# Four two-bank PSUM tiles in a ring with dependencies by bank, and attention visits of four and three chunks, in a fused sigmoid-attention and SwiGLU kernel

## The chip, the cores and the metric

One core of a Trainium2 chip. The metric is the time on the device in microseconds (us), start of the program to its end. Each timed version was run several times, interleaved with the kernel before on the same chip.

## The reference

Sigmoid attention over 8 batches, 12 heads, 448 positions and head dimension 64, followed by a gated feed-forward block (FFN) on the 3584 tokens.

```python
scores = q @ k.T / sqrt(64) - log(448)          # per batch and head
attn   = 1 / (1 + exp(-scores))
x      = (attn @ v)  -> [3584, 768]
g      = x @ w_gate                             # 768 -> 1536
out    = (g * sigmoid(g) * (x @ w_val)) @ w_out # 1536 -> 768
```

## The kernel before

The instruction order is fixed by the program; the framework only adds the semaphores. Of the engines, TensorE does the matmuls and transposes, ScalarE (ACT in the views) the sigmoids, VectorE (DVE) the copies and products. xT is the attention output in the layout that the FFN reads, T the transposed q and k. Words used below: a *head group* n is four heads of one batch (24 groups, three to a batch). Its scores come in seven *chunks* c. A *QK tile* is the scores of one chunk: four matmuls on 64x64 tiles of the array, side by side. *PV* is the product with v of a whole group. An *FFN unit* is one gate product and one value product of six matmuls each, or the output products of one block of 128 tokens (twice twelve matmuls). Before, a visit may also fall between the two halves of a unit (the kinds g, v and o in the loop below are halves); after, only between whole units. TensorE does FFN units most of the time and breaks off for a *visit* to attention. One trip from FFN to attention and back is called a *trip*.

PSUM, the memory that TensorE writes its results to, has eight banks. Before, four of them are two score tiles of two banks, and four are single tiles that everything else shares:

```python
psA = tile_pool(name="psA", bufs=2, space=PSUM)      # score tiles, two banks each
psG = tile_pool(name="psG", bufs=4, space=PSUM)      # one bank each

def qk_tile(n, c):
    sc = psA.tile([128, 2, 512], FP32, tag="A", name="ps_sc")
    # ... four 64x64 matmuls: two halves w, two heads h2
    return sc

def sig_tile(n, c, sc):
    pt = ptp.tile([128, 2, S], FP16, tag="pt", name="pt")
    nc.scalar.activation(out=pt, in_=sc[:, :, :S], func=SIGM, bias=sb_t, scale=qkscale)

def pv(n):
    P = [psG.tile([128, S], FP32, tag="G", name=f"ps_pv{w}") for w in range(2)]
    # ... 28 64x64 matmuls, then four VectorE copies to the two xT tiles of the group

def trans_pe(n, which):                               # q or k of one group, seven transposes
    ps = psG.tile([128, C, 128], BF16, tag="G", name="ps_tr")
    # ... seven transposes, then one VectorE copy to T

def ffn1(b, f, gate):                                 # gate or value product of one unit
    ps = psG.tile([128, S], FP32, tag="G", name="ps_g" if gate else "ps_vl")
    # ... six matmuls; gate: ScalarE sigmoid s16, VectorE t1 = ps*s16; value: VectorE hT = ps*t1
# ... ffn2: twelve matmuls, one VectorE copy to osb, then a store
```

The order of the visits, and the main loop:

```python
tiles  = [(n, c) for n in range(NJ, NQ) for c in range(C)]     # C = 7, NJ = 3, NQ = 24
visits = [tiles[i:i + 2] for i in range(0, len(tiles), 2)]     # two QK tiles to a visit

def attn_step(group, pvs):
    scs = [(n, c, qk_tile(n, c)) for n, c in group]
    for n in pvs:
        pv(n)
    for n, c, sc in scs:
        sig_tile(n, c, sc)

for dur, u in units:                       # FFN work, in order
    while vi < len(visits) and tcur >= vtime[vi]:
        group = visits[vi]; vi += 1
        attn_step(group, pvs)              # pvs: groups whose last chunk is done
        for n, c in group:
            if c == 1:
                nn = n + 2
                if loaded <= nn + 1 < NQ:
                    load3(nn + 1)          # q, k, v of a later group
                if casted <= nn < NQ:
                    cast(nn, 0, nc.gpsimd); cast(nn, 1, nc.gpsimd)
                    # ... DMA transposes from group 6 on, cast of v
            if c == 5 and n + 1 < NPE:     # NPE = 6
                trans_pe(n + 1, 0); trans_pe(n + 1, 1)
    # ... one FFN unit of kind g, v or o
    tcur += dur
```

Batch 0 has no FFN to mix with: its 21 QK tiles, sigmoids and three PV run first, while weights still load in four blocks of the gate and of the value matrix.

Of the kernel before, what the change touches and what calls it, by code (L numbers as in the profile page):

```python
# [17 lines left out]
def kernel(  # L18
# [10 lines left out]
    nc = tc.nc  # L29
# [17 lines left out]
    psA = ctx.enter_context(tc.tile_pool(name="psA", bufs=2, space=bass.MemoryType.PSUM))  # L47
    psG = ctx.enter_context(tc.tile_pool(name="psG", bufs=4, space=bass.MemoryType.PSUM))
# [14 lines left out]
    make_identity(nc, idn)  # L63

# [51 lines left out]
    def trans_pe(n, which):  # L116
        t = q16.pop((n, which))
        ps = psG.tile([128, C, 128], BF16, tag="G", name="ps_tr")
        for c in range(C):
            nc.tensor.transpose(  # L120
                out=ps[:, c, :], in_=t[:, c].rearrange("p h d -> p (h d)"), identity=idn
            )
        d = qkT.tile([128, C, 128], BF16, tag=f"T{which}", name=f"T{which}_{n}")
        nc.vector.tensor_copy(out=d, in_=ps)  # L124
        qT[(n, which)] = d
# [5 lines left out]
    def qk_tile(n, c):  # L131
        sc = psA.tile([128, 2, 512], FP32, tag="A", name="ps_sc")
        qt, kt = qT[(n, 0)], qT[(n, 1)]
        for w in range(2):
            for h2 in range(2):
                r = slice(h2 * 64, h2 * 64 + 64)
                nc.tensor.matmul(  # L137
                    out=sc[w * 64:(w + 1) * 64, h2, :S],
                    lhsT=kt[r, c, w * 64:(w + 1) * 64],
                    rhs=qt[r, :, w * 64:(w + 1) * 64],  # L140
                    start=True,
                    stop=True,
                )
        return sc
# [6 lines left out]
    def pv(n):  # L151
        b, j = divmod(n, NJ)
        P = [psG.tile([128, S], FP32, tag="G", name=f"ps_pv{w}") for w in range(2)]
        vt = v16.pop(n)
        for c in range(C):
            pt = pts.pop((n, c))
            for h2 in range(2):
                for w in range(2):
                    r = slice(w * 64, w * 64 + 64)
                    nc.tensor.matmul(  # L160
                        out=P[w][h2 * 64:(h2 + 1) * 64, :],
                        lhsT=vt[r, h2, c * D:(c + 1) * D],
                        rhs=pt[r, h2, :],
                        start=(c == 0),
                        stop=(c == C - 1),
                    )
        for h2 in range(2):
            x = xtp.tile([128, S], FP16, tag="xT", name=f"xT_{b}_{2 * j + h2}")
            for w in range(2):
                nc.vector.tensor_copy(  # L170
                    out=x[w * 64:(w + 1) * 64, :], in_=P[w][h2 * 64:(h2 + 1) * 64, :]
                )
            xT[(b, 2 * j + h2)] = x
        qT.pop((n, 0))
        qT.pop((n, 1))
# [3 lines left out]
    gcur = {}  # L179

    def ffn1(b, f, gate):
        ps = psG.tile([128, S], FP32, tag="G", name="ps_g" if gate else "ps_vl")
        w = (wg16 if gate else wv16)[f // FW]
        cs = slice((f % FW) * 128, (f % FW) * 128 + 128)
        for pr in range(NP):
            nc.tensor.matmul(  # L186
                out=ps, lhsT=w[:, pr, cs], rhs=xT[(b, pr)], start=(pr == 0), stop=(pr == NP - 1)
            )
        if gate:
            s16 = tmp.tile([128, S], FP16, tag="s16", name="s16")  # L190
            nc.scalar.activation(out=s16, in_=ps, func=SIGM)  # L191
            t1 = tmp.tile([128, S], FP16, tag="t1", name="t1")
            nc.vector.tensor_tensor(out=t1, in0=ps, in1=s16, op=MULT)  # L193
            gcur[0] = t1
        else:
            if b % 2 == 0:
                hT[(b // 2, f)] = htp.tile([128, 2, S], FP16, tag="hT", name=f"hT_{b // 2}_{f}")
            nc.vector.scalar_tensor_tensor(  # L198
                out=hT[(b // 2, f)][:, b % 2, :], in0=ps, scalar=HSC, in1=gcur[0], op0=MULT, op1=MULT
            )  # L200

    osb_cur = {}

    def ffn2(b, m, half):
        hw = DM // 2
        if half == 0:
            osb_cur[0] = osp.tile([128, DM], FP32, tag="osb", name="osb")
        osb = osb_cur[0]
        o = psG.tile([128, hw], FP32, tag="G", name="ps_o")
        for f in range(NF):  # L210
            h = hT[(b // 2, f)].rearrange("p b s -> p (b s)")
            lhsT = h[:, m * 128:(m + 1) * 128]
            nc.tensor.matmul(  # L213
                out=o,
                lhsT=lhsT,
                rhs=wo16[f // FW][:, f % FW, half * hw:(half + 1) * hw],
                start=(f == 0),
                stop=(f == NF - 1),
            )
        nc.vector.tensor_scalar(  # L220
            out=osb[:, half * hw:(half + 1) * hw], in0=o, scalar1=HREC, scalar2=None, op0=MULT
        )
        if half == 1:
            for i in range(2):
                bb, c = divmod(2 * m + i, C)
                bb += b - b % 2
                dst = out[bb * S:(bb + 1) * S, :].rearrange("(p c) n -> c p n", c=C)[c]
                nc.gpsimd.dma_start(out=dst, in_=osb[i * 64:(i + 1) * 64, :])  # L228


    FU1, FU2 = 1.13, 1.95
# [3 lines left out]
    for pb in range(B // 2):  # L235
        for b in (2 * pb, 2 * pb + 1):
            f1_start[b] = tt
            for f in range(NF):
                units.append((FU1, ("g", b, f)))
                units.append((FU1, ("v", b, f)))  # L240
                tt += 2 * FU1
            f1_end[b] = tt
        for m in range(7):
            for half in range(2):
                units.append((FU2, ("o", 2 * pb + (m > 2), m, half)))
                tt += FU2
# [3 lines left out]
    tiles = [(n, c) for n in range(NJ, NQ) for c in range(C)]  # L250
    visits = [tiles[i:i + 2] for i in range(0, len(tiles), 2)]
# [10 lines left out]
    def attn_step(group, pvs):  # L262
        scs = [(n, c, qk_tile(n, c)) for n, c in group]
        for n in pvs:
            pv(n)
        for n, c, sc in scs:
            sig_tile(n, c, sc)
# [15 lines left out]
    trans_pe(0, 0)  # L283
    trans_pe(0, 1)
# [6 lines left out]
    for n, c in b0:  # L291
        attn_step([(n, c)], [n - 1] if c == 2 and n > 0 else [])
        if (n, c) == (0, 3):
            trans_pe(1, 0)
            trans_pe(1, 1)
# [5 lines left out]
        if (n, c) == (1, 3):  # L301
            trans_pe(2, 0)
            trans_pe(2, 1)
# [6 lines left out]
        if (n, c) == (2, 3):  # L310
            trans_pe(3, 0)
            trans_pe(3, 1)
# [13 lines left out]
    pend = []  # L326
    for dur, u in units:
        while vi < len(visits) and tcur >= vtime[vi]:
# [4 lines left out]
            for n, c in group:  # L333
# [18 lines left out]
                if c == 5 and n + 1 < NPE:  # L352
                    trans_pe(n + 1, 0)
                    trans_pe(n + 1, 1)
        if pend and (u[0] == "g" and u[2] == 0 and (u[1], NP - 1) not in xT or vi == len(visits) and tcur >= vtime[-1] + 4.0):
# [3 lines left out]
        if u[0] == "g":  # L359
            ffn1(u[1], u[2], True)  # L360
        elif u[0] == "v":
            ffn1(u[1], u[2], False)
        else:
            ffn2(*u[1:])
# [31 lines left out]
```

## Time and profile before

| | before |
|---|---|
| median of 3 runs | 449.37 us (448.82 to 450.17) |
| span of the profiled execution | 446.4 us |
| TensorE busy | 94% |
| VectorE, ScalarE busy | 49%, 47% |
| trips from FFN to attention and back | 74 |

The prediction shows the page's busy line, its DMA row, the chain of waits and two visits in order of time. In the page, one digit of a row is a fortieth of the span (11 us) in tenths. Here is the granted TensorE clock over the slices:

```profile
PEclk9899999999999999999999999999999999999998
```

The second digit of the clock row is an 8: in the second slice TensorE ran part of the time at half clock (from 19.3 to 22.7 us). The view by stretches of time says how slow (columns: stretch; its length; busy time of each engine with the number of instructions; granted clock; DMA share; GB/s):

```profile
19.30:22.60 3.30, 3.02 (x36) 1.79 (x35) 0.00 (x0) 2.02 (x3) 0.90 (x2) 0.50 1.17 285
```

The clock was 0.50 there.

### The profile page before, as it was taken

How to read it: one execution, taken by the hardware profiler on the slowest of the kernel's cores; microseconds unless marked ns; L12 is line 12 of the kernel's file. 1: busy time of each engine (PE TensorE's matmuls, PEld its weight loads, DVE VectorE, ACT ScalarE, POOL GpSimd, SP SyncE). 2: the span in 40 equal slices, each digit the busy share in tenths (PEclk: the TensorE clock that was granted, in tenths of full speed). 3: DMA queues.
4: the chain of work that ended last, by engine and by line, in shares of the span. 5: the costliest groups of instructions: out<-in, count | busy, mean ns of one | idle time of the engine just before them, and what ended most of it. 6: DMA issues, size and time to landing. Idle time of an engine off the chain costs nothing.

```text
span 446.4 us, 7870 instructions
## 1 busy us (share of the span) xinstructions
PE 420.9 (94%) x3252; PEld 212.2 (48%) x3252; DVE 220.1 (49%) x360; ACT 210.9 (47%) x267; POOL 100.7 (23%) x142
## 2 busy tenths in 40 slices
PE   2678999999999999999999999999999999999992
PEld 1344444444555444444555444444555545555661
DVE  1265665466334456556424546646524446555231
ACT  3887675655533655565444464565444441221000
POOL 1764140220234512000324612200021100000221
PEclk9899999999999999999999999999999999999998
DMA  8999999994284986500278694220033300000242
GB/s 264 332 286 286 182 249 196 232 280 149 58 249 94 262 248 167 164 1 1 50 222 231 135 302 134 42 42 3 0 82 87 79 4 1 1 1 0 72 106 70
DMA packets 63587, 59.88 MB, mean 134 GB/s; under 512 B 35648, under 2 KB 61760, under 8 KB 63552
## 3 DMA queue, kind: packets, MB, share of 16 engines
q1 hardware_dynamic: 52992, 41.30, 34.8%
q0 software_dynamic: 10560, 18.09, 19.3%
q8 instruction: 25, 0.41, 0.4%
q14 instruction: 10, 0.08, 0.1%
HBM read 47.19 MB, written 11.01 MB: 130 GB/s over the span
## 4 chain that ended last, share of the span: by engine, by line
PE 92%; ACT 2%; DMA 2%; DVE 1%; issue 1%; POOL 0%; SPq 0%; POOLq 0%; ACTq 0%
PE ps_o L213 25%; PE ps_vl L186 25%; PE ps_g L186 25%; PE ps_sc L137 9%; PE ps_pv L160 7%; ACT pt L148 2%; DMA st<-in_q_dram 2%; PE ps_tr L120 1%; DVE xT L170 1%; SPq L88 0%; POOL c L108 0%; DVE osb L220 0%; POOL out_dram L228 0%; POOLq L391 0%; ACTq L148 0%
## 5 line engine op out<-in xcount | busy, mean ns | idle before, releaser
L148 ACT ACTIVATE pt<-ps_sc,sb_t 128x896 f16<-128x896 f32 x168 | 159.6, 1005 | 88.5 <-PE ps_sc L137 88.5
L186 PE MATMUL ps_g<-xT,wg 128*128 128x448 f16 x576 | 125.4, 353 | 1.5 <-DVE xT L170 1.4
L186 PE MATMUL ps_vl<-xT,wv 128*128 128x448 f16 x576 | 124.9, 353 | 0.0
L213 PE MATMUL ps_o<-wo,hT 128*128 128x384 f16 x672 | 113.5, 326 | 0.0
L193 DVE TENSOR_TENSOR t<-ps_g,s 128x448 f16<-128x448 f32 x96 | 59.9, 624 | 84.7 <-ACT s L191 84.1
L191 ACT ACTIVATE s<-ps_g 128x448 f16<-128x448 f32 x96 | 52.2, 544 | 103.2 <-PE ps_g L186 103.2
L213 PEld LDWEIGHTS <-hT 128*128 128x128 f16 x672 | 64.0, 98 | 48.6 <-issue 7.9
L186 PEld LDWEIGHTS <-wv 128*128 128x128 f16 x576 | 54.3, 98 | 58.6 <-issue 10.7
L186 PEld LDWEIGHTS <-wg 128*128 128x128 f16 x576 | 54.1, 98 | 57.0 <-issue 9.7
L228 POOL DMA_DIRECT2D out_dram<-osb x56 | 29.3, 528 | 211.2 <-DVE osb L220 211.0
L170 DVE CAST xT<-ps_pv 64x448 f16<-64x448 f32 x96 | 59.7, 622 | 30.8 <-PE ps_pv L160 29.4
L198 DVE SCALAR_TENSOR_TENSOR hT<-ps_vl,t 128x448 f16<-128x448 f32 x96 | 60.0, 625 | 16.6 <-PE ps_vl L186 8.5
L220 DVE TENSOR_SCALAR osb<-ps_o 128x384 f32<-128x384 f32 x56 | 31.2, 558 | 74.6 <-PE ps_o L213 74.4
L137 PE MATMUL ps_sc<-T,T 64*64 64x448 bf16 x672 | 51.1, 370 | 8.8 <-ACT pt L148 7.2
L108 POOL CAST c<-st 128x896 bf16<-128x896 f32 x43 | 39.7, 939 | 54.7 <-DMA st<-in_q_dram 30.3
L108 POOL CAST v<-st 128x896 f16<-128x896 f32 x24 | 22.6, 942 | 72.8 <-PE ps_pv L160 52.9
L160 PE MATMUL ps_pv<-pt,v 64*64 64x448 f16 x672 | 37.5, 359 | 0.3 <-ACT pt L148 0.3
L137 PEld LDWEIGHTS <-T 64*64 64x64 bf16 x672 | 13.7, 106 | 39.7 <-issue 37.1
L160 PEld LDWEIGHTS <-v 64*64 64x64 f16 x672 | 20.8, 109 | 12.8 <-issue 0.9
L120 PE MATMUL ps_tr<-idn,c 128*128 128x128 bf16 x84 | 7.3, 250 | 6.5 <-DVE c L108 4.7
L120 PEld LDWEIGHTS <-c 128*128 128x128 bf16 x84 | 5.9, 113 | 8.8 <-DVE c L108 4.7
L124 DVE COPY T<-ps_tr 128x896 bf16<-128x896 bf16 x12 | 7.1, 620 | 5.4 <-PE ps_tr L120 5.2
(14 smaller groups left out, 17.2 us busy)
## 6 DMA issues: line engine op xcount, KB each, us to landing
st<-in_q_dram SPq DMA_DIRECT2D x24, 448.0 KB, 4.5
st<-in_k_dram SPq DMA_DIRECT2D x24, 448.0 KB, 5.9
st<-in_v_dram SPq DMA_DIRECT2D x24, 448.0 KB, 7.3
out_dram<-osb POOLq DMA_DIRECT2D x56, 192.0 KB, 3.1
wg<-in_moe_w_gate_dram POOLq DMA_DIRECT2D x4, 576.0 KB, 24.8
wv<-in_moe_w_val_dram POOLq DMA_DIRECT2D x4, 576.0 KB, 29.7
wo<-in_moe_w_out_dram POOLq DMA_DIRECT2D x4, 576.0 KB, 35.4
T<-c SPq DMA_TRANSPOSE x36, 3.2
```

Source lines behind the costliest of these rows:

```text
L108: eng.tensor_copy(out=o, in_=i)
L137: nc.tensor.matmul(out=sc[w * 64:(w + 1) * 64, h2, :S], lhsT=kt[r, c, w * 64:(w + 1) * 64], rhs=qt[r, :, w * 64:(w + 1) * 64], start=True, ...
L148: nc.scalar.activation(out=pt, in_=sc[:, :, :S], func=SIGM, bias=sb_t, scale=qkscale)
L160: nc.tensor.matmul(out=P[w][h2 * 64:(h2 + 1) * 64, :], lhsT=vt[r, h2, c * D:(c + 1) * D], rhs=pt[r, h2, :], start=(c == 0), stop=(c == C - 1),
L170: nc.vector.tensor_copy(out=x[w * 64:(w + 1) * 64, :], in_=P[w][h2 * 64:(h2 + 1) * 64, :])
L186: nc.tensor.matmul(out=ps, lhsT=w[:, pr, cs], rhs=xT[(b, pr)], start=(pr == 0), stop=(pr == NP - 1))
L191: nc.scalar.activation(out=s16, in_=ps, func=SIGM)
L193: nc.vector.tensor_tensor(out=t1, in0=ps, in1=s16, op=MULT)
L198: nc.vector.scalar_tensor_tensor(out=hT[(b // 2, f)][:, b % 2, :], in0=ps, scalar=HSC, in1=gcur[0], op0=MULT, op1=MULT)
L213: nc.tensor.matmul(out=o, lhsT=lhsT, rhs=wo16[f // FW][:, f % FW, half * hw:(half + 1) * hw], start=(f == 0), stop=(f == NF - 1),)
L220: nc.vector.tensor_scalar(out=osb[:, half * hw:(half + 1) * hw], in0=o, scalar1=HREC, scalar2=None, op0=MULT)
L228: nc.gpsimd.dma_start(out=dst, in_=osb[i * 64:(i + 1) * 64, :])
```

## The change

The intent: fewer trips. A visit of four or three QK tiles needs more than two score tiles, so the eight banks become four persistent two-bank tiles, used in turn by everybody (a ring). A user of a whole tile would hold two banks longer than needed, so users declare which bank each matmul writes and each reader reads, and a declared pair on different banks isn't ordered.

```diff
-    psA = ctx.enter_context(tc.tile_pool(name="psA", bufs=2, space=bass.MemoryType.PSUM))
-    psG = ctx.enter_context(tc.tile_pool(name="psG", bufs=4, space=bass.MemoryType.PSUM))
+    psD = ctx.enter_context(tc.tile_pool(name="psD", bufs=1, space=bass.MemoryType.PSUM))
...
+    ring = [psD.tile([128, 2, 512], FP32, tag=f"D{i}", name=f"ps_D{i}") for i in range(4)]
...
+    class Banked:
+        def __init__(self, user=None):          # takes the next tile of the ring
...
+        def write(self, ins, bank):
+            if bank is not None:
+                self.has_mm[bank] = True
+                tc.add_to_no_dep_group(self.mm[bank], ins.ins)
+                p = self.prev
+                if p is not None and p.has_rd[1 - bank] and not (self.user == "o" and p.user == "f"):
+                    tc.declare_no_dep(ins.ins, group=p.rd[1 - bank], reason="the other bank")
+        def read(self, ins, bank):
+            if bank is not None:
+                if self.has_mm[1 - bank]:
+                    tc.declare_no_dep(ins.ins, group=self.mm[1 - bank], reason="the other bank")
+                self.has_rd[bank] = True
+                tc.add_to_no_dep_group(self.rd[bank], ins.ins)
...
-        sc = psA.tile([128, 2, 512], FP32, tag="A", name="ps_sc")
+        sc = Banked().t
...
-        P = [psG.tile([128, S], FP32, tag="G", name=f"ps_pv{w}") for w in range(2)]
+        P = Banked().t
...
-    def ffn1(b, f, gate):
+    def ffn1(b, f):                             # gate and value in one tile, one bank each
+        D = Banked("f")
+        for i, w16 in enumerate((wg16, wv16)):
+            for pr in range(NP):
+                D.write(nc.tensor.matmul(out=D.t[:, i, :S], ...), i)
...
-    tiles = [(n, c) for n in range(NJ, NQ) for c in range(C)]
-    visits = [tiles[i:i + 2] for i in range(0, len(tiles), 2)]
+    visits = [[(n, c) for c in cs] for n in range(NJ, NQ) for cs in (range(4), range(4, C))]
...
     def attn_step(group, pvs):
-        scs = [(n, c, qk_tile(n, c)) for n, c in group]
-        for n in pvs:
-            pv(n)
-        for n, c, sc in scs:
-            sig_tile(n, c, sc)
+        for part in (group[:2], group[2:]):
+            scs = [(n, c, qk_tile(n, c)) for n, c in part]
+            while pvs:
+                pv(pvs.pop(0))
+            for n, c, sc in scs:
+                sig_tile(n, c, sc)
...
-                if c == 5 and n + 1 < NPE:
-                    trans_pe(n + 1, 0)
-                    trans_pe(n + 1, 1)
+                if c == 4 and n + 1 < NPE:
+                    post.append(n + 1)          # its transposes come after the next FFN unit
...
+        fn(*args)
+        while post:
+            trans_pe(post.pop())
```

(The bodies of ffn1, ffn2 and trans_pe are cut; each now writes both banks of one tile. The loops of the `D.write` call are shortened.) The score tiles declare nothing: their one sigmoid reads both banks.

## The prediction

> **What bounds the kernel now.** I read the page first (busy shares, chain), then the waits, then the order of time around single visits of attention. The page's busy line, the DMA row of its slices and the first line of the chain of work that ended last:
>
> ```profile
> PE 420.9 (94%) x3252; PEld 212.2 (48%) x3252; DVE 220.1 (49%) x360; ACT 210.9 (47%) x267; POOL 100.7 (23%) x142
> DMA  8999999994284986500278694220033300000242
> ...
> PE 92%; ACT 2%; DMA 2%; DVE 1%; issue 1%; POOL 0%; SPq 0%; POOLq 0%; ACTq 0%
> ```
>
> TensorE is busy or next in line almost throughout; the other engines are half idle. The DMA engines are saturated in slices 2 to 9 (11 us each), which matters below. So the change can win only TensorE idle time, and PE's busy share hides that. I therefore took the start times of all 3252 matmuls and compared neighbours. At full clock the pitch is 189 ns for a 128x448 matmul, 162.5 ns for 128x384, 189 ns for four 64x64 ones side by side, 56 ns for a transpose. Count times pitch gives 395.1 us. From the first matmul at 4.7 us to the last at 437.7 us lie 38.0 us more. Where they are, by the waits:
>
> ```profile
> PEld L137 <- issue: 37.1, 88, 2.5
> PEld L186 <- issue: 20.4, 54, 1.2
> ...
> PE ps_sc L137 <- ACT pt L148: 7.2, 10, 2.1
> ...
> PE ps_g L186 <- DVE xT L170: 1.4, 2, 0.9
> ```
>
> PE hardly waits for another engine; what recurs is "issue" before the first weight load after a change of matmul kind. Two visits in order of time, one with PV and one without:
>
> ```profile
> 152.88 0.14 PEld L137 LDWEIGHTS <-T 64*64 64x64 bf16 x8 [0.37 <-issue]
> 152.88 0.57 PE L137 MATMUL ps_sc<-T,T 64*64 64x448 bf16 x8
> ...
> 153.28 1.49 PE L160 MATMUL ps_pv<-pt,v 64*64 64x448 f16 x28
> 153.31 1.91 ACT L148 ACTIVATE pt<-ps_sc,sb_t 128x896 f16<-128x896 f32 x2 [0.92 <-PE ps_sc L137]
> ...
> 154.70 0.87 PEld L186 LDWEIGHTS <-wg 128*128 128x128 f16 x6 [0.36 <-issue]
> ...
> 154.82 2.54 DVE L170 CAST xT<-ps_pv 64x448 f16<-64x448 f32 x4 [1.04 <-PE ps_pv L160]
> ...
> 162.23 0.14 PEld L137 LDWEIGHTS <-T 64*64 64x64 bf16 x8 [0.37 <-issue]
> ...
> 162.73 0.87 PEld L186 LDWEIGHTS <-wg 128*128 128x128 f16 x6 [0.36 <-issue]
> ```
>
> Start to start, every visit, whatever is in it, costs 0.220 to 0.222 us beyond its matmuls: 0.094 going into 64x64 tiles, the rest coming out. There are 74 such FFN-to-attention-to-FFN trips from 38 us on: 16.35 us. One more stall lies there, 0.635 us at 76.5 us (the gate of batch 1 waits for the copies of xT). The remaining idle time is the start, before the first FFN tile.
>
> **What the Trainium skill says.** "TensorEngine Tiling (Array Packing)", Tiling Modes, Key Properties: changing the tiling mode, not just the tile, drains TensorE. The trace agrees: 0.22 us per round trip between 128x128 and 64x64, and nothing between QK and PV, which share the mode. "PSUM — Partial Sum Buffer", PSUM bank collisions: semaphores should guard PSUM by bank and quadrant; an engine may read one bank while PE writes another. The kernel before does just that with one-bank FFN tiles, so waiting by bank buys nothing over it, it only keeps what two-bank tiles would lose. The skill's first page ("Trainium Kernel Development and Optimization", Key Constraints) says that DMAs from all queues run on the same 16 engines and interleave; the saturated slices agree (332 GB/s in the best), so weights asked for earlier don't land earlier.
>
> **The change, part by part.**
> PSUM: before, two 2-bank score tiles and four 1-bank tiles; after, four 2-bank tiles used strictly in turn by QK, PV, FFN and transposes. The instruction counts per kind are the same; only order and waits move. The order of the built program shows 42 visits in place of 74. (Both also have one lone PV at the end, and in both the first visit has no FFN before it: so 74 trips before, 42 after.)
>
> 1. *Trips removed.* From 68.2 us on (why there, see 3) before has 64 trips, 14.13 us. After has the two visits of each of 18 head groups and one PV alone, 37 x 0.221 = 8.18 us. Saved 5.95 us, all on PE's path.
>
> 2. *A new wait.* A visit with PV now takes slots in the order QK0, QK1, PV, QK2, QK3, and the next FFN unit gets the slot four users back: that of QK1. The built program's semaphore says the same: that unit's first matmul waits for the sigmoid of QK1. Count from the visit's first QK matmul. In the trace above the sigmoid of QK0 starts at 0.436 (153.314-152.878), that of QK1 0.906 later, and ends 1.00 after that: 2.34. A released matmul starts 0.05 us after an activation's end (startup: 16.829 to 16.881). So the FFN can start at 2.39. Without the wait it would start at 1.829 (154.707-152.878) plus two more QK tiles, 2 x 0.189: 2.207. The wait is 0.187 us. QK3 itself needs QK0's sigmoid, done at 1.44, and PE gets there at 1.89: free. The second FFN unit takes PV's slot; the four copies end at 4.48 (157.362-152.878), release at 4.53, and PE arrives at 2.39+2.27=4.66: free, by only 0.13. QK2 needs the previous unit's last DVE read, done at 0.90, PE arrives at 1.70. The visit without PV meets slots read long before; its next FFN unit needs the gate product of the unit just before, ready about 0.3 after that unit's end, and three QK tiles take 0.79. So 18 x 0.187 = 3.37 us given back.
>    The 0.635 us stall for xT goes, since the visit before it is longer and PV follows earlier: 0.64 saved.
>
> 3. *The start.* Four score slots let QK run ahead of the sigmoids. The sigmoids of batch 0 are 21 x 0.9 = 19 us from 11.1 us on but end at 34.2 before, having waited for QK behind transposes and behind a PV at half clock. Without such waits they would end at 11.1+19 = 30.1; the ring still makes some wait for DVE's copies, so I put them near 31: about 3 us gained. But this gain is lost again, to weights. The loads of the value weights:
>
> ```profile
> L78 POOL DMA_DIRECT2D wv<-in_moe_w_val_dram x4: 826/827/845, 12.9 to 30.8; - x4
> ...
> DMA to landing us min/median/max: 18.5/29.7/36.3
> ```
>
>    The last value block lands at 30.8+36.3 = 67.1; the third at 56.4 by its semaphore. Before, their first users start at 68.22 and 57.75: margins of 1.1 and 1.4 us. After, even with no gain at the start, the third block's user would arrive at 55.9 and wait until 56.44. From there 1.14 (rest of the unit) + 0.78 (transposes) + 2.49 (visit with PV and its wait) + 4.54 (two units) + 0.79 (visit) + 1.14 (gate half) reach the last block's user at 67.3, just past its landing. So of everything that happens before 68 us, 68.22-67.3 = 0.9 us survives.
>
> Sum: 0.9 + 5.95 + 0.64 - 3.37 = 4.1 us. Against the median, 449.4-4.1 = 445.3 us, 0.9% faster. The tail is the same work as before.
>
> **The rivals.**
> *The ring stalls more than I count.* One order for all users couples PE to the slowest reader. For it: the 0.13 us margin behind PV's copies, and ScalarE gets four sigmoids in a row, so the next gate's sigmoid starts 0.3 us late. Against it: that lateness falls on a slot needed four users on, 5 us later, and DVE and ACT are about half idle. Each extra 0.2 us per visit with PV costs 3.6 us: 449, a draw.
> *No wait at all at the visits, or a cheaper one.* If PE is slower coming out of 64x64 mode, or the sigmoid is released sooner, the 3.37 us stay: 441.9. Against it: the wait adds measured stamps of one visit, and ACT is free there.
> *The start's gain survives.* If the weights land earlier because casts and loads move up, another 1 to 2 us: 443 to 444; with the previous rival 440. Against it: saturated DMA slices. The opposite is also possible: PE idling for weights for 1 to 2 us could let its clock drop. "TensorE: Matmul & The Clock Gate", Part 1, gives free-running activity windows of some 3.4 us; this trace has one at half clock from 19.3 to 22.7 us, after thinly spread QK work. Such a window costs up to 1.7 us: 447.
>
> **Range and chances.** The trips saved are near certain, so the range hangs on the new wait (0 to 0.4 us, 18 times) and the start (0 to 2.5 us). 443.0 to 447.8 should hold it 8 times in 10. Two per cent faster is under 440.4, which needs both kind rivals at once: 0.04. Two per cent slower is over 458.4, which needs over 0.7 us of extra wait at each of 18 visits: 0.02. Within: 0.94.
>
> **What would show it.** Right: PE's trips fall to 42, each still 0.22; at the FFN unit after each visit with PV, a PE wait for the sigmoid of about 0.19, 18 to 20 times, 3 to 4 us in the waits; sigmoids of batch 0 ending near 31 us; PE waiting for the third and second value blocks near 45 and 56 us; no wait for xT near 76. Wrong: waits of PE for DVE's xT copies at the second unit (then the margin of 0.13 failed), waits before QK2 or QK3, value weights landing before 55 or after 58 us, or a second half-clock window past 35 us.

## The result and the profile after

Ratios are computed as the mean time of one kernel's runs over the mean of the other's of the same rounds, so they aren't quite ratios of the medians quoted.

| | before | after |
|---|---|---|
| median (4 runs each) | 449.19 us (448.82 to 450.17) | 445.60 us (445.16 to 446.48) |
| ratio, 95% interval | | 0.9919, 0.9897 to 0.9941 |
| span of the profiled execution | 446.4 us | 443.9 us |
| trips | 74 | 42 |

It is 0.8% faster, 3.6 us by the medians. Predicted were 445.3 us and 4.1. A repeat with six runs of the unchanged changed kernel (told below) gave 445.49. The page after, busy line, clock row and the chain (in the lines of this kernel L182 is QK, L205 PV, L231 the FFN's gate and value products, L193 the score sigmoid, L162 the transposes and L169 their copies; other kernels number them a little differently):

```profile
PE 413.1 (93%) x3252; PEld 218.4 (49%) x3252; DVE 220.7 (50%) x360; ACT 208.6 (47%) x267; POOL 100.5 (23%) x142
...
PEclk9999999999999999999999999999999999999998
...
PE 75%; DMA 14%; ACT 5%; issue 2%; POOL 2%; DVE 1%; SPq 0%; POOLq 0%; ACTq 0%; DVEq 0%
```

The chain has changed: DMA was 2% of it and is 14% (9 of these are the value weights, by the chain's second line). That is the first sign that weights now stop TensorE. (The same 3252 matmuls count 7.8 us less busy than before, more than the kernel gained: their ends are modelled, so the busy share does not measure TensorE's work.) The waits after (columns: engine, line, what it waited for; us in total, times, longest):

```profile
PEld L182 <- issue: 20.6, 48, 2.3
...
PE ps_D L231 <- DMA wv<-in_moe_w_val_dram: 3.9, 3, 1.9
...
PE ps_D L182 <- DVE T L169: 2.3, 3, 1.0
...
PE ps_D L231 <- ACT pt L193: 0.4, 2, 0.2
```

"issue" before the first QK weight load of a visit was 37.1 us in 88 cases before and is 20.6 in 48: most of that are the trips that went. New are three waits for value weights and up to 1.0 us for DVE's copies of the transposes. One visit with PV, in order of time (columns: start; busy; engine, line, operation, tiles and count; idle before and its releaser):

```profile
266.53 0.57 PE L182 MATMUL ps_D<-T,T 64*64 64x448 bf16 x8
...
266.93 1.49 PE L205 MATMUL ps_D<-pt,v 64*64 64x448 f16 x28
266.96 3.70 ACT L193 ACTIVATE pt<-ps_D,sb_t 128x896 f16<-128x896 f32 x4 [0.92 <-PE ps_D L182]
...
268.73 1.04 PEld L231 LDWEIGHTS <-wg 128*128 128x128 f16 x6 [0.36 <-issue]
268.92 1.29 PE L231 MATMUL ps_D<-xT,wg 128*128 128x448 f16 x6
```

From the first QK matmul to the first FFN matmul are 268.92 - 266.53 = 2.39 us. The prediction had 2.39 with the new wait and 2.207 without it. Note how badly the wait shows: the weight load before it says only "issue 0.36", as it does in visits that don't wait, and the waits list has none of it, except for the fourth line shown above and a like one at the output units (two cases each, 0.8 us together). These are the four visits where ScalarE had been idle and began its first sigmoid 0.50 us after QK's start, not 0.436. I had to take the start times of all matmuls, as for the prediction. Excess over the matmuls' own pitch, start to start:

| visit | before | after |
|---|---|---|
| without PV | 0.219 to 0.221 us | 0.220 to 0.221 us |
| with PV | 0.221 to 0.222 us | 0.406 to 0.409 us, four of 0.466 to 0.469 (the lone PV at the end: 0.221) |

So the new wait is 0.187 us. The second FFN unit did not wait for PV's copies, and the 0.635 us for xT at 76.5 us is gone.

To tell the start from the rest, I took one mark in every trace: the first value matmul of the last weight block. Time from the mark to the last matmul:

| | mark at | mark to last matmul |
|---|---|---|
| before, first profile and repeat | 68.15, 69.61 us | 369.58, 369.59 us |
| after, first profile and repeat | 68.99, 69.00 us | 366.25, 366.24 us |

From the mark on, the change gave 3.33 to 3.34 us, and this part repeats to 0.01 us; predicted were 5.95 + 0.64 - 3.37 = 3.22. The agreement is in part luck. By the start times the visits gave 14.126 - 11.762 = 2.36 us (2.58 predicted; the four of 0.466 make the difference) and the xT stall 0.64. One QK tile more lies behind the mark in the changed kernel, which takes 0.19 back, and 0.52 us came from gaps of at most 0.011 us between FFN matmuls, 0.82 us in all before and 0.30 after, which nobody predicted and nothing here explains. Before the mark there is no dependable gain: against the first profile of before the changed kernel was 0.8 us later, against the second 0.6 earlier. The timed medians, 3.6 us, leave some 0.3 us for it. Predicted were 0.9.

Where does the start's gain go? The changed kernel began its first FFN matmul at 33.04 us (before 34.90). Then:

```profile
56.62 1.31 PE L231 MATMUL ps_D<-xT,wv 128*128 128x448 f16 x6 [1.90 <-DMA wv<-in_moe_w_val_dram]
57.76 0.94 PE L162 MATMUL ps_D<-idn,c 128*128 128x128 bf16 x14
...
58.51 1.15 DVE L169 COPY T<-ps_D 128x896 bf16<-128x896 bf16 x2
...
59.70 0.57 PE L182 MATMUL ps_D<-T,T 64*64 64x448 bf16 x8 [1.00 <-DVE T L169]
```

TensorE waits for a value block (1.90 us here, 1.71 at 44.45 us, both as predicted), and then for something not predicted: the transposes of group 5 lie directly before the QK tiles that need them, so QK waits for DVE's two copies. Start to start it cost 1.07 us. The change itself put them there. The kernel before has them directly behind a visit, with a whole unit between them and their QK, which waits for nothing:

```profile
55.66 0.95 PE L120 MATMUL ps_tr<-idn,c 128*128 128x128 bf16 x14
...
58.82 0.57 PE L137 MATMUL ps_sc<-T,T 64*64 64x448 bf16 x8
```

### The profile page after: what moved, and what is told of

Its sections match the earlier page's. It is cut to its first block, busy times and chain, and to the rows that moved or that the text cites. A ratio compares the mean times of both kernels' runs of the same rounds, so it can differ in the third digit from the quotient of the medians.

```text
span 443.9 us, 7927 instructions
## 1 busy us (share of the span) xinstructions
PE 413.1 (93%) x3252; PEld 218.4 (49%) x3252; DVE 220.7 (50%) x360; ACT 208.6 (47%) x267; POOL 100.5 (23%) x142
## 4 chain that ended last, share of the span: by engine, by line
PE 75%; DMA 14%; ACT 5%; issue 2%; POOL 2%; DVE 1%; SPq 0%; POOLq 0%; ACTq 0%; DVEq 0%
PE ps_D L231 44%; PE ps_D L258 25%; DMA wv<-in_moe_w_val_dram 9%; ACT pt L193 5%; PE ps_D L182 4%; DMA st<-in_v_dram 3%; DMA st<-in_q_dram 2%; PE ps_D L205 2%; POOL v L147 1%; DVE t L240 0%; DVE hT L244 0%; POOL wg L117 0%; ACT s L238 0%; SPq L127 0%; POOL c L147 0%
## 5 line engine op out<-in xcount | busy, mean ns | idle before, releaser
L193 ACT ACTIVATE pt<-ps_D,sb_t 128x896 f16<-128x896 f32 x168 | 156.0, 1008 | 91.7 <-PE ps_D L182 91.7
L231 PE MATMUL ps_D<-xT,wv 128*128 128x448 f16 x576 | 124.7, 353 | 3.9 <-DMA wv<-in_moe_w_val_dram 3.9
L231 PE MATMUL ps_D<-xT,wg 128*128 128x448 f16 x576 | 124.8, 353 | 1.8 <-ACT pt L193 0.4
L258 PE MATMUL ps_D<-wo,hT 128*128 128x384 f16 x672 | 111.7, 326 | 0.8 <-ACT pt L193 0.4
L240 DVE TENSOR_TENSOR t<-ps_D,s 128x448 f16<-128x448 f32 x96 | 59.8, 623 | 89.3 <-ACT s L238 87.7
L238 ACT ACTIVATE s<-ps_D 128x448 f16<-128x448 f32 x96 | 52.6, 548 | 101.1 <-PE ps_D L231 95.2
L231 PEld LDWEIGHTS <-wv 128*128 128x128 f16 x576 | 56.1, 98 | 57.2 <-DMA wv<-in_moe_w_val_dram 5.2
L231 PEld LDWEIGHTS <-wg 128*128 128x128 f16 x576 | 54.8, 98 | 59.1 <-issue 11.3
L215 DVE CAST xT<-ps_D 64x448 f16<-64x448 f32 x96 | 59.7, 622 | 30.4 <-PE ps_D L205 29.4
L269 DVE TENSOR_SCALAR osb<-ps_D 128x384 f32<-128x384 f32 x56 | 31.2, 558 | 72.9 <-PE ps_D L258 72.1
L244 DVE SCALAR_TENSOR_TENSOR hT<-ps_D,t 128x448 f16<-128x448 f32 x96 | 60.0, 625 | 12.5 <-PE ps_D L231 2.3
L182 PE MATMUL ps_D<-T,T 64*64 64x448 bf16 x672 | 47.0, 366 | 7.3 <-DVE xT L215 4.3
L205 PE MATMUL ps_D<-pt,v 64*64 64x448 f16 x672 | 36.1, 350 | 1.6 <-ACT pt L193 1.0
L182 PEld LDWEIGHTS <-T 64*64 64x64 bf16 x672 | 16.4, 107 | 29.8 <-issue 20.6
L205 PEld LDWEIGHTS <-v 64*64 64x64 f16 x672 | 20.1, 107 | 14.2 <-issue 3.0
L162 PE MATMUL ps_D<-idn,c 128*128 128x128 bf16 x84 | 7.5, 249 | 7.0 <-DVE c L147 4.9
L162 PEld LDWEIGHTS <-c 128*128 128x128 bf16 x84 | 6.2, 111 | 9.3 <-DVE c L147 5.2
L169 DVE COPY T<-ps_D 128x896 bf16<-128x896 bf16 x12 | 7.1, 620 | 2.4 <-PE ps_D L162 2.3
```

Of the source, the lines that this page charges most:

```text
L182: nc.tensor.matmul(out=sc[w * 64:(w + 1) * 64, h2, :S], lhsT=kt[r, c, w * 64:(w + 1) * 64], rhs=qt[r, :, w * 64:(w + 1) * 64], start=True, ...
L205: nc.tensor.matmul(out=P[h2 * 64:(h2 + 1) * 64, w, :S], lhsT=vt[r, h2, c * D:(c + 1) * D], rhs=pt[r, h2, :], start=(c == 0), stop=(c == C ...
L215: nc.vector.tensor_copy(out=x[w * 64:(w + 1) * 64, :], in_=P[h2 * 64:(h2 + 1) * 64, w, :S])
L231: nc.tensor.matmul(out=D.t[:, i, :S], lhsT=w16[f // FW][:, pr, cs], rhs=xT[(b, pr)], start=(pr == 0), stop=(pr == NP - 1),),
L238: D.read(nc.scalar.activation(out=s16, in_=D.t[:, 0, :S], func=SIGM), 0)
L240: D.read(nc.vector.tensor_tensor(out=t1, in0=D.t[:, 0, :S], in1=s16, op=MULT), 0)
```

## The experiments

Ratios are to the kernel before in the same rounds. Its medians were 449.06 us with experiments 1 to 4, 449.02 with 5 to 8 and 449.35 with 9 to 12. Experiments 1 to 8 ran on one chip, 9 to 12 on another, so times of the two groups are compared by their ratios.

The record has the mean granted clock of every timed run, also of those without a trace. In the fourteen profiled executions it tells how many half-clock stretches of 3.4 us there were: 0.995 to 0.997 with none, 0.991 to 0.993 with one, 0.987 with two (0.994, which none of them has, is counted as none below). It doesn't tell where they lay.

### 1. Release the score tile by halves

Theory: the 0.187 us are a wait of the FFN unit's gate for the whole sigmoid of QK1. If that sigmoid becomes two instructions, one per bank, each declared to its bank, the gate can start after the first.

```diff
-    def sig_tile(n, c, sc):
+    def sig_tile(n, c, D, split=False):            # qk_tile returns the Banked object
         pt = ptp.tile([128, 2, S], FP16, tag="pt", name="pt")
-        nc.scalar.activation(out=pt, in_=sc[:, :, :S], func=SIGM, bias=sb_t, scale=qkscale)
+        if split:
+            for i in range(2):
+                D.read(nc.scalar.activation(out=pt[:, i, :], in_=D.t[:, i, :S],
+                                            func=SIGM, bias=sb_t, scale=qkscale), i)
+        else:
+            nc.scalar.activation(out=pt, in_=D.t[:, :, :S], func=SIGM, bias=sb_t, scale=qkscale)
     def attn_step(group, pvs):
+        split = bool(pvs) and len(group) == 4
...
-                sig_tile(n, c, sc)
+                sig_tile(n, c, sc, split and c == 1)
```

> The changed kernel, with the sigmoid of QK1 in each visit with PV cut in two, one instruction for each PSUM bank, and the next FFN unit's gate waiting for the first alone. Theory (the 0.187 us at these visits is the wait for the whole sigmoid of QK1): the first half ends about 0.4 us earlier, the gate no longer waits, a visit with PV costs 0.22 us beyond its matmuls in place of 0.407, and the second unit now meets the 4.53 us release of PV's slot 0.06 us early: 18 x 0.187 less some 12 x 0.06 = 2.6 us, so 445.6 - 2.6 = 443.0 us (3.4 us, 442.2, if that second wait doesn't come). Rival (the extra is TensorE's own cost of a longer visit with PV between two lots of QK): still 0.407 us, 445.6 us.

Measured: 441.24 us (440.66 to 444.45, 6 runs), ratio 0.9849 (0.9813 to 0.9885), result correct. The visit of above, now in this kernel:

```profile
263.19 0.57 PE L183 MATMUL ps_D<-T,T 64*64 64x448 bf16 x8
...
264.53 1.15 ACT L197 ACTIVATE pt<-ps_D,sb_t 128x448 f16<-128x448 f32 x2
...
264.92 0.55 PE L183 MATMUL ps_D<-T,T 64*64 64x448 bf16 x8
...
265.40 1.31 PE L241 MATMUL ps_D<-xT,wg 128*128 128x448 f16 x6
```

Two ScalarE instructions of half the size take the place of one, and QK to FFN is 265.40 - 263.19 = 2.21 us in place of 2.39. All visits with PV after the mark are back at 0.222 us. Because TensorE arrives earlier at the second unit, 14 of these units (12 after the mark) now wait 0.043 to 0.047 us for PV's copies: the 0.13 us margin of the prediction less the 0.187 us gained is -0.06. From the mark to the end the kernel takes 363.40 us, 2.85 less than the changed one. This settles the new wait: mechanism and size. About 1.5 us more than that came from before the mark. In the profiles the mark came 1.41 us earlier (67.58 in place of 68.99): 0.86 because the third value block landed at 55.7 us in place of 56.6, 0.42 because the last one (65.8 in place of 68.9) wasn't waited for, and 0.13 from the split itself. Nothing shows that the split made the blocks land earlier: the unchanged repeat (experiment 11) has them at 54.1 and 63.5 us.

### 2 and 3. Take the weights' arrival away

Theory: the start's gain is lost to the landing of the weights. In both kernels all weight blocks of the gate and the value are made block 0, which lands first. The result is wrong (relative error 1.2253).

```diff
-    wg16 = [one.tile([128, NP, FW * 128], FP16, tag=f"wg{i}", name=f"wg16_{i}") for i in range(NW)]
-    wv16 = [one.tile([128, NP, FW * 128], FP16, tag=f"wv{i}", name=f"wv16_{i}") for i in range(NW)]
+    wg16 = [one.tile([128, NP, FW * 128], FP16, tag="wg0", name="wg16_0")] * NW
+    wv16 = [one.tile([128, NP, FW * 128], FP16, tag="wv0", name="wv16_0")] * NW
...
     def w_load(kind, i):
+        if kind != "o" and i > 0:
+            return
```

> The changed kernel, wrong on purpose: only the first block of the gate and value weights is loaded, and all FFN units use it. Same instructions on TensorE, six weight loads of 576 KB x 2 fewer. Theory (before 69 us it is the landing of the value weights that sets the pace, and eats what the start gained): the three waits of 1.87, 2.07 and 0.42 us go, 4.4 us in all, 441.2 us. Rival (the start itself, or the clock, sets the pace there): no more than 1 us faster, 444.6 to 445.6 us.

> The kernel before, with the same edit, wrong on purpose. Theory (there the weights land 1.1 to 2 us ahead of their use, so nothing waits for them): within 0.5 us of the kernel before, 448.7 to 449.7 us. So the changed kernel would be ahead of it by 8 us where weights are no limit, against 3.6 us where they are. Rival (the saturated DMA slows the start of both alike): as much faster as the changed kernel with this edit, 4 us, 445 us.

Measured: changed kernel 444.94 us (443.04 to 446.36, 6 runs), ratio 0.9912 (0.9881 to 0.9944); kernel before 447.81 us (446.55 to 449.92, 6 runs), ratio 0.9982 (0.9950 to 1.0014), nothing that its interval tells from zero. The theory falls short: with no weights to wait for, the changed kernel gains hardly anything, as the rival had it. The trace says what took their place:

```profile
57.20 0.62 DVE L242 TENSOR_TENSOR t<-ps_D,s 128x448 f16<-128x448 f32 x1 [2.75 <-ACT s L240]
...
58.47 1.15 DVE L171 COPY T<-ps_D 128x896 bf16<-128x896 bf16 x2
...
59.67 0.57 PE L184 MATMUL ps_D<-T,T 64*64 64x448 bf16 x8 [2.25 <-DVE T L171]
...
60.08 2.33 PE L207 MATMUL ps_D<-pt,v 64*64 64x448 f16 x28
```

TensorE waits 2.25 us for the copies of the transposes. These stand on VectorE behind the two products of the FFN unit just before, and the first product waits for ScalarE's gate sigmoid; only then come the copies. Then the PV takes 2.33 us in place of 1.49: half clock, as the view by stretches shows for this run.

```profile
60.60:64.00 3.40, 3.40 (x35) 1.40 (x24) 1.52 (x3) 2.59 (x4) 0.93 (x1) 0.50 1.07 287
```

The clock is 0.50 there, and also from 29.9 to 33.3 us: two stretches of 3.4 us, each worth up to half of that, 1.7 us (an estimate). So there are two limits one behind the other: weights, and the transposes' place in the order. My second theory: both have to go.

### 4. The ring alone

Rival: the gain is the ring's, not the visits'. The changed kernel with the old visits of two QK tiles:

```diff
-    visits = [[(n, c) for c in cs] for n in range(NJ, NQ) for cs in (range(4), range(4, C))]
+    tiles = [(n, c) for n in range(NJ, NQ) for c in range(C)]
+    visits = [tiles[i:i + 2] for i in range(0, len(tiles), 2)]
...
-                if c == 4 and n + 1 < NPE:
+                if c == 5 and n + 1 < NPE:
```

> One part of the change alone: the ring of four two-bank tiles with waits by bank and undivided FFN units, but the 74 visits of two chunks of the kernel before. Theory (the ring by itself gives nothing past the start, the visits saved are the gain): trips cost 0.22 us 74 times again, no wait for the sigmoid of QK1 since the next unit then gets the slot of an FFN unit, 448.5 to 449.3 us. Rival (the ring's freer slots are the gain): 446 us or less.

Measured: 450.85 us (449.30 to 451.84, 6 runs), ratio 1.0044 (1.0016 to 1.0072). The rival falls: with 74 trips of 0.22 us the ring costs time. From the mark to the end it needs 371.69 us, 2.1 more than before. In the trace are stalls for xT of 0.65 and 1.11 us between 78 and 81 us (0.635 in one place before) and one boundary at which two visits fell together, four QK in a row with 0.83 us. Expected were 448.5 to 449.3 us, no slower than before: the stalls were not foreseen.

### 5. The visits alone

The kernel before, with its old pools, and the new visits:

```diff
-    tiles = [(n, c) for n in range(NJ, NQ) for c in range(C)]
-    visits = [tiles[i:i + 2] for i in range(0, len(tiles), 2)]
+    visits = [[(n, c) for c in cs] for n in range(NJ, NQ) for cs in (range(4), range(4, C))]
...
     def attn_step(group, pvs):
-        scs = [(n, c, qk_tile(n, c)) for n, c in group]
...
+        for part in (group[:2], group[2:]):
+            scs = [(n, c, qk_tile(n, c)) for n, c in part]
+            while pvs:
+                pv(pvs.pop(0))
+            for n, c, sc in scs:
+                sig_tile(n, c, sc)
```

> The other part of the change alone: visits of four chunks with PV and three without, on the PSUM pools of the kernel before (two 2-bank score tiles, four 1-bank tiles). Theory (the larger visits need the ring's third and fourth score slot): the third chunk of a visit waits for the sigmoid of the first. Without PV that is 1.49 us after the visit's start where TensorE is ready at 0.38: 1.11 us, 21 times. With PV the fourth chunk waits for the sigmoid of the second, 2.39 against 1.89: 0.5 us, 20 times. 33 us of new waits against 7.1 us of saved trips: 449 + 26 = 475 us, 470 to 480. Rival (the visits alone give the gain, the ring is not needed): 442 to 446 us.

Measured: 476.60 us (476.25 to 476.81, 4 runs), ratio 1.0619 (1.0581 to 1.0657). A line of its waits, and the fourth QK tile of a visit:

```profile
PE ps_sc L137 <- ACT pt L148: 36.3, 53, 2.1
```

```profile
166.03 0.38 PE L137 MATMUL ps_sc<-T,T 64*64 64x448 bf16 x4 [0.31 <-ACT pt L148]
```

With two score tiles, each further QK waits for a sigmoid of about 1 us: 36.3 us in 53 cases. Visits without PV cost 1.34 to 1.44 us each, with PV 0.72 to 0.83; expected were 0.22 with 1.11 and with 0.5 us of waits, that is 1.33 and 0.72. The change is of the kind where neither half is worth anything alone: the ring pays nothing, the visits pay only with the ring.

### 6. The ring without the declarations by bank

```diff
         def write(self, ins, bank):
+            return
...
         def read(self, ins, bank):
+            return
```

> The changed kernel without its declarations by bank: each wait is for the whole two-bank tile. The built program then has the gate's sigmoid wait for the value matmuls and the next user of a slot for the last of its readers. Theory: after each visit without PV the next FFN unit waits for the last product of the unit just before, ready at 1.98 us after the visit's start where TensorE is ready at 0.69: 1.3 us at some 15 visits and 0.6 at 6 between output units; visits with PV lose 0.3 to 0.5 us more: 20 + 4 + 7 = about 28 us, 473 us, 465 to 480. Rival (four slots are enough for whole-tile waits): within 2 us of the changed kernel.

Measured: 470.88 us (470.52 to 472.34, 4 runs), ratio 1.0498 (1.0464 to 1.0532). A visit without PV:

```profile
155.30 0.76 PE L184 MATMUL ps_D<-T,T 64*64 64x448 bf16 x12
155.41 0.54 ACT L240 ACTIVATE s<-ps_D 128x448 f16<-128x448 f32 x1 [4.62 <-PE ps_D L233]
...
156.64 0.62 DVE L246 SCALAR_TENSOR_TENSOR hT<-ps_D,t 128x448 f16<-128x448 f32 x1
...
157.32 1.30 PE L233 MATMUL ps_D<-xT,wg 128*128 128x448 f16 x6 [1.26 <-DVE hT L246]
```

The gate's sigmoid starts only after the whole unit (155.41, after the value's last matmul), so the chain sigmoid, product, product ends at 157.26, and the next unit, whose slot this is, waits for it: 1.546 us for this visit (expected 0.22 + 1.3). The declarations are thus worth 470.9 - 445.6 = 25 us in this ring. They keep the ring from losing to the one-bank tiles of before, as the prediction had it.

### 7. Weights aliased and the transposes first

Second theory: put the transposes before the FFN unit in place of after it, as in the kernel before, so that DVE's copies lie beside that unit. First without weights to wait for (wrong result), so that nothing else is in the way:

```diff
-        fn(*args)
         while post:
             trans_pe(post.pop())
+        fn(*args)
```

> The changed kernel with one block of gate and value weights for all units (wrong on purpose, as before), and with TensorE's transposes of the next head group placed before the FFN unit they follow in the changed kernel. The run with the weights alone taken away came to 444.9, not 441.2: its trace has QK waiting 2.3 us at 57 us for VectorE's copies of transposes issued just before it, and a half-clock window of 3.4 us right after. Theory (two limits in a row at the start: weights, then these copies): with both gone 444.9 - 2.3 - up to 1.7 for the clock: 441.5 us, 440.5 to 442.5. Rival (a third limit takes their place): 444 us or more.

Measured: 441.52 us (440.14 to 442.72, 6 runs), ratio 0.9833 (0.9804 to 0.9862): as expected to 0.1 us, and 3.4 us under experiment 2, from the order of two statements: in the trace the 2.25 us wait and the half-clock stretch behind it are gone (the one at 30 us is still there). The mark comes at 66.51 us and the rest takes 366.24 us, as in the changed kernel. Of the 3.4 us about 2.4 seem to be the wait and the rest clock: the one timed run of experiment 2 with no stretch (clock 0.997) took 443.04 us, the two of this one (0.995 and 0.996) 441.10 and 440.14. So with both limits gone the start's gain survives: mark 2.5 us earlier.

### 8. A correct version: split, order of transposes, order of loads

To get weights in time without aliasing, the loads of q, k and v of later groups are issued after the DMA transposes of the group before, which come later in time, so that they compete less with the weights on the full DMA engines. With the split of experiment 1 and the order of experiment 7:

```diff
                     nn = n + 2
-                    if loaded <= nn + 1 < NQ:
-                        load3(nn + 1)
-                        loaded = nn + 2
                     if casted <= nn < NQ:
...
                         casted = nn + 1
+                    if loaded <= nn + 1 < NQ:
+                        load3(nn + 1)
+                        loaded = nn + 2
```

> A correct candidate for the best of all: the split sigmoid of QK1, the transposes before the FFN unit, and the loads of q, k and v for head groups 7 and later queued behind the DMA transposes of the group before, so that the weights have the DMA engines more to themselves from 40 to 67 us. Theory: the split gives 441.2 as measured; the weights' and copies' waits cost 5.4 us in the changed kernel's trace, of which most goes: 437 to 438.5 us, 2.5% under the kernel before. Rival (the weights land no earlier, or the later loads of q, k and v are missed elsewhere): 441 us or more.

Measured: 438.73 us (437.13 to 440.11, 6 runs), ratio 0.9769 (0.9740 to 0.9799), correct, and the only version over 2% faster than before (expected 437 to 438.5). The value blocks land at 31.2, 42.9, 51.5 and 61.0 us, in the changed kernel at 31.0, 44.4, 56.6 and 68.9. That the loads' move does this is borne out by the other traces: with it (experiments 8, 9 and 10) the third block lands at 48.4 to 51.5 us and the last at 58.3 to 61.0, in the eight traces of all four blocks without it at 54.1 to 57.1 and 63.5 to 69.6. The same place in the order, in this kernel:

```profile
52.96 0.95 PE L162 MATMUL ps_D<-idn,c 128*128 128x128 bf16 x14
53.57 1.16 DVE L169 COPY T<-ps_D 128x896 bf16<-128x896 bf16 x2 [0.34 <-PE ps_D L162]
...
53.76 1.30 PE L241 MATMUL ps_D<-xT,wg 128*128 128x448 f16 x6
...
56.12 0.57 PE L183 MATMUL ps_D<-T,T 64*64 64x448 bf16 x8
```

The copies end at 54.73 beside the FFN unit, and QK at 56.12 waits for nothing. The mark comes at 64.85 us.

### 9. The two moves without the split, and 10. the loads' move on the kernel before

Experiment 9 is experiment 8 without the split; experiment 10 is the kernel before with `load3` moved as in 8. The edits are those shown.

> The changed kernel with the two moves of order alone (transposes before the FFN unit, loads of q, k and v for head groups 7 and later behind the DMA transposes), without the split sigmoid. Theory (the order's gain and the split's are separate stretches of TensorE's time and add up): the candidate with both, 438.7, plus 20 visits x 0.187 less 14 x 0.043 = 3.1 us: 441.8 us, 441 to 442.6; no wait for value weights in its trace. Rival (the split gained at the start as well, or the order alone does little): 444 us or more.

> The kernel before with the later loads of q, k and v, its other order untouched. Theory (it has no wait for weights to lose): 448.3 to 449.5 us, within 0.7 us of the kernel before. Rival (the lighter DMA traffic helps every version): 446 to 447 us.

Measured: experiment 9, 443.32 us (441.18 to 443.95, 6 runs), ratio 0.9857 (0.9820 to 0.9894), correct, 1.5 us slower than expected (0.9 by the ratios, since it ran on another chip than experiment 8: 0.0088 of 449 us is 3.95, and 3.1 were expected). Experiment 10, 448.18 us (446.59 to 449.84, 6 runs), ratio 0.9976 (0.9940 to 1.0013), nothing that its interval tells from zero: the loads' move by itself is no gain to the kernel before. No run has the transposes' move alone with all the weights loaded, so how much of the gain of 8 and 9 each of the two moves brings is not shown.

Where is this rest? No wait for value weights is in its trace (blocks land by 58.3 us). But TensorE waits once for PV's copies, and its FFN then begins at half clock (a line in order of time, then one of the view by stretches):

```profile
34.53 0.38 PE L182 MATMUL ps_D<-T,T 64*64 64x448 bf16 x4 [2.06 <-DVE xT L215]
```

```profile
35.10:38.30 3.20, 3.20 (x10) 1.37 (x9) 0.49 (x1) 1.47 (x2) 2.35 (x3) 0.50 1.17 283
```

and here the same stretch in experiment 8:

```profile
35.10:38.30 3.20, 3.20 (x19) 1.66 (x17) 1.25 (x2) 1.30 (x3) 2.37 (x3) 1.00 1.17 286
```

Ten matmuls against 19 in the same 3.2 us. The split touches only visits of four QK tiles with PV, and the first of these starts at 45 us, so up to there experiments 8 and 9 are the same program (on two chips): whether a half-clock stretch falls there isn't set by the edit. The marks are 67.10 and 64.85 us, 2.25 apart: two split visits before the mark explain 0.37 less 0.09 of waits for PV's copies, an earlier start of the FFN 0.30 (34.55 in place of 34.85 us), and the 1.7 left are what a half-clock stretch costs. Experiment 8 had the same wait of 2.06 us and ran at full clock after it; its own half-clock stretch lay at 22.5 to 25.9 us, where the sigmoids set the pace. So the profiled executions add up. By the mean clock the timed runs agree: all six of experiment 9 lie at 0.991, one stretch each, and of experiment 8 four at 0.994 or 0.995, none, and two at 0.991. Where the untraced stretches lay, and whether the other chip has a part in it, is not shown.

### 11 and 12. Both kernels again, unchanged

> The changed kernel unaltered, a second profile and more times. If the landing of the value weights sets the pace before 69 us, the last block's first user starts within 0.1 us of that landing or of the copies' wait before it, while the visits from 69 us on cost the same 0.407 and 0.22 us as in the first profile: 445.2 to 446 us. If the first profile was a chance, other waits.

> The kernel before unaltered, as a control for the chip's own spread: ratio to itself 1.000 with an interval of some 0.3%, 448.7 to 449.5 us; visits at 0.22 us again, and the spread of single runs (446.6 to 450.4 so far) made before 40 us, since everything after is the same to 0.1 us.

Measured: the changed kernel 445.49 us (445.10 to 447.08, 6 runs), ratio 0.9921 (0.9889 to 0.9953); before 448.91 us (447.09 to 449.93, 6 runs), ratio 0.9992 (0.9958 to 1.0026). In this trace of the changed kernel the last value block landed at 63.5 us, 5.4 us earlier than in the first one, and yet the mark came at 69.00:

```profile
60.13 0.57 PE L182 MATMUL ps_D<-T,T 64*64 64x448 bf16 x8 [2.26 <-DVE T L169]
```

QK of group 5 waited 2.26 us for the copies, and from 34.4 to 37.8 us lay a half-clock stretch. Three limits (weights, transposes' copies, clock) stand in for one another; that both traces show the same mark to 0.01 us is chance. In the second trace of before the last block landed at 69.6 us and the mark came at 69.61: there before itself waited for its weights.

## Why the prediction was right, and where it wasn't

The time (445.3 predicted, 445.6 measured) and "less than 2% faster" were right, in part by luck: the start gave less than predicted, and the rest more. By its steps:

1. *Trips removed, 5.95 us:* right. 42 trips, each of unchanged cost but for the new wait.
2. *The new wait, 0.187 us:* right in mechanism and size, and settled by experiment 1, which removes it with one instruction more per visit. The four cases of 0.466 us are the only addition to this term. The margins: PV's copies held, as said, and failed by 0.045 us once experiment 1 brought TensorE there sooner.
3. *The stall for xT:* gone. The three terms together were 3.22 predicted and 3.00 measured; the 3.33 to 3.34 from the mark on hold other things besides, as told above.
4. *The start, 0.9 us:* the term that was mis-sized. The step that failed is "0.78 (transposes) + 2.49 (visit with PV and its wait)": it counts transposes and then QK with nothing between. In the kernel before a whole unit lay between them, and the change took it away. The runs showed a wait for DVE's copies there of 1.07 us start to start (in the views, which count from the modelled end of the matmul before, 1.00, and 2.25 and 2.26 us in experiments 2 and 11). In the first profile the third block also landed 0.18 us later (56.62 in place of 56.44): 67.3 + 1.07 + 0.18 = 68.55, against the 68.57 at which TensorE reached the last block's user, and that block landed at 68.9, not 67.1. So the mark was at 68.99. Experiments 2 and 7 settle that the copies bound the start behind the weights: taking away the weights alone gave nothing worth naming, and moving the transposes as well gave 3.4 us, some 2.4 of it at like clock. The 0.9 us predicted came out as about 0.3 by the medians and is not above the spread of the start.
5. *"I put them near 31":* batch 0's sigmoids ended at 29.7 us, so the gain put at stake at the start was larger (the first value matmul came 3.2 us earlier, 1.1 of them because the kernel before waits for xT inside its first unit); it was lost just the same.
6. *The signs to look for:* "3 to 4 us in the waits" was wrong about the view, not the wait: the waits list shows 0.8 us of it in four cases. The wait for the third and second value blocks, and the absence of the xT wait, came as said. Two signs of being wrong came true in the repeat alone: the third block landed before 55 us (54.1), and a half-clock stretch reached past 35 us (34.4 to 37.8). The time was the same.

The rival "the start's gain survives" failed because of the order inside the changed kernel, not because it is impossible: experiment 8 has it. The rival with the lost clock was partly right: half-clock stretches past 34 us occur in some executions (experiments 2, 9 and 11), not in the first profile.

What stays open: why the blocks landed earlier in experiment 1's profile than in the changed kernel's first one, and whether its timed runs gained in the same way. The clock alone doesn't say: five of the six runs of experiment 1 had no half-clock stretch (0.994 to 0.996), but the three of the ten of the changed kernel that had none (445.3 to 446.5 us) were no faster than the others. Also open: what decides whether a half-clock stretch follows a wait.

## What to carry to other kernels

Batching the visits of a minority mode saves a fixed price per switch, but it needs buffers for the longer visit: changing only the schedule or only the buffers lost 6% and 0.4% here. When a buffer ring is shared, work out for every user whose slot it takes and when that slot's last reader ends, to a hundredth of a microsecond; a reader can be split so that half of the slot comes free early. And before counting a gain at the start of a kernel, look for the next limits behind the first: a producer placed directly before its consumer (here the transposes) can take much of the gain.

## What the Trainium skill lacked or had wrong

- "TensorEngine Tiling (Array Packing)" says that a mode switch drains TensorE and gives no figure. Here a trip from 128x128 to 64x64 matmuls and back costs 0.219 to 0.222 us start to start, 0.094 of it on the way in, and nothing between QK and PV, which are both 64x64.
- "TensorE: Matmul & The Clock Gate", Why this matters for your kernels, advises to have no idle gaps of TensorE over some 3 us. Here half-clock stretches of 3.41 us (the page's window length agrees) followed single waits of 2.06 us (experiments 9, 11) and 2.25 us (experiment 2), or QK work spread thin (before, 19.3 to 22.7 us). So the length of the gap decided it in neither direction: the first profile of the changed kernel and experiments 1 and 8 had the same wait of 2.06 us and full clock after it, and experiment 4 had a wait of 3.06 us for weights (to 57.13 us) and full clock after it. Where TensorE sets the pace a stretch costs up to 1.7 us (half of 3.41, an estimate), against 3.6 us for the whole change.
- No page has a figure of what ordering PSUM users by bank is worth. In a ring of two-bank tiles it is 25 us of 471 (experiment 6).
- No page warns that a wait of TensorE of under 0.2 us after a mode switch can go unseen in a list of waits: 14 of the 18 waits after 69 us, of 0.187 us each, were not listed, and they made 2.6 us.
